# Five SBUF homes in place of three for the output tiles of a fused linear-attention and channel-mix kernel

## The chip, the core and the metric

The kernel runs on one NeuronCore of a Trainium2 chip. The metric is the device time of one launch in microseconds, the median of several runs. TensorE is called PE here (its weight loads PEld), VectorE DVE, ScalarE ACT, GpSimd POOL and SyncE SP. A trailing q (SPq, DVEq) marks work of an engine's sequencer: it waits or issues DMAs while the engine itself stays idle.

## The reference

Eight batches, eight heads, 576 positions, 64 numbers per head. An attention of linear kind feeds a channel mix:

```python
q_s = softmax(q, over the head's 64)
k_s = softmax(k, over the 576 positions)
x   = q_s @ (k_s^T @ v)                    # heads side by side: [8, 576, 512]
x_prev = x, one position later, 0 in front
xk = mu_k * x + (1 - mu_k) * x_prev
xr = mu_r * x + (1 - mu_r) * x_prev
k  = maximum(xk @ w_k, 0)                  # 512 -> 1024
v  = (k * k) @ w_v                         # 1024 -> 512
out = sigmoid(xr @ w_r) * v                # float32
```

## The kernel before

**Tiling.** `attention(b, g)` makes x for one batch and four heads. Exponentials (ACT, L454), sums and reciprocals (DVE, L467 and L470) and the scaling of q (DVE, L475) prepare its inputs. One block on PE, in tiles of 64x64, then transposes q (L507), forms the product of keys and values (L484, into a PSUM tile `att`) and multiplies q with the product of the block before it (L520). Between them DVE takes the reciprocal of the key sums (`rz`, L492), copies the transposed q out of PSUM (`qt`, L512) and scales the product into weights (`w`, L605); ACT copies x out in two pieces (`xb`, L614 and L617); DVE shifts, scales and mixes it (L622 to L636) into `xk` and `xr`, two bf16 rings of four batches.

The channel mix runs in units of 512 positions, the last of each half 256 (`unit`, L694). For each of eight slices of the 1024 hidden numbers, PE multiplies `xk` with `w_k` into one of four PSUM banks `mm_a` to `mm_d` (`k_part`, L722), ACT takes the RELU (`rel`, L706) and DVE squares it into `k2` (L710; the pages write k_a, k_b). Then, for each 128 positions, PE makes the gate's argument from `xr` and `w_r` (`r_part`, L756), ACT its tanh into a tile `th` (L761), and PE the value from `k2` and `w_v` in two halves of four matmuls (`v_part`, L766). DVE's `gated` (L772) adds 1 to the tanh and multiplies with the value in PSUM: it writes one output tile `ot` of 128 x 512 float32, 2 KB per partition, and by that sets the PSUM bank free. `store` (L783) sends the tile to HBM in two DMAs of 64 rows, 128 KB each, on SP's queue. There are 36 output tiles; the last is made and stored in two column halves, so 37 instructions are at L772.

**Order.** Nothing is ordered by a scheduler on the chip. `Plan` holds every operation with its engine, an estimated duration, what it depends on, and which buffers it takes and sets free. `Plan.order` books one operation at a time: for each engine, the one that can start first among those whose inputs are ready, and among those that can start within a look-ahead the one due first. Lead times such as `EARLY` are set by hand. The resulting order is emitted as it is, and each engine works through its queue in that order. Semaphore waits are put in for each dependence: on data, and on a buffer that an earlier reader still holds. An instruction with several things to wait for gets extra wait instructions ahead of it (EVENT_SEMAPHORE).

**Homes.** Each buffer family has a number of places, listed in `pools`. When an operation takes one, `slot_time` gives the place whose last user ends first:

```python
late = [o.end for o in user.last]
free = None if not late or None in late or free is None else max(
    [free] + late)
...
if free is not None and (best is None or free < best[0]):
    best = (free, i)
```

For `ot` the last users are the tile's stores. In the trace the homes `ot_a`, `ot_b` and `ot_c` are used in turn. So each `gated` waits on the chip until both DMAs of the tile three before it have landed, and DVE, which works in order, waits with it. The operations of SP in this phase are the stores alone; POOL issues the loads of q, k and v (`raw`, L310), the last of them at 98.95 us.

Of the kernel before, what the change touches and what calls it, by code (L numbers as in the profile page):

```python
# [208 lines left out]
def kernel(  # L209
# [25 lines left out]
    assert B % 4 == 0  # L235

    pools = {"raw": 12, "eq": 3, "ek": 2, "vv": 2, "stat": 4, "qs": 2, "qt": 3, "w": 3, "wp": 4,
             "rz": 3, "xb": 2, "xd": 2, "xm": 3, "k2": 2, "rel": 3, "th": 2, "ot": 3, "mm": 4,
             "att": 2, "early": 2}
    shared = {("early", i): [("mm", 2 * i), ("mm", 2 * i + 1)] for i in range(2)}  # L240
    plan = Plan(pools, shared)
# [620 lines left out]
```

## Time and profile before

Five runs: 201.1 to 202.66 us, median 202.21. The profiled execution took 201.58 us; its span, from the first instruction to the last, is 199.8 us. The granted PE clock was full (1.00) throughout.

| stretch, us | length | PE busy | DVE busy | ACT busy | POOL busy | DMA, GB/s |
|---|---|---|---|---|---|---|
| 0 to 20 | 20.0 | 9.88 | 12.84 | 12.00 | 10.44 | 261 |
| 20 to 95 | 75.0 | 73.91 | 67.34 | 65.08 | 29.04 | 358 |
| 95 to 112 | 17.0 | 16.26 | 15.03 | 12.31 | 1.44 | 195 |
| 112 to 187 | 75.0 | 74.21 | 61.04 | 43.78 | 0.00 | 57 |
| 187 to 199.8 | 12.8 | 8.72 | 4.56 | 3.96 | 0.00 | 83 |

A row gives the time in which each engine was busy within the stretch, and the mean rate of all DMAs. Up to about 105 us the loads of q, k, v and the weights share the DMA engines with the stores; after that only stores are left.

| stores (L783), each 128 KB | least | median | most |
|---|---|---|---|
| issue to landing, 30 to 110 us | 3.2 | 6.2 | 8.6 |
| issue to landing, 110 to 200 us | 2.2 | 2.4 | 3.7 |

A DMA's landing is the moment at which its semaphore has its full count. Times of matmuls overlap their neighbours' in the records, as they are pipelined and their ends are modelled; distances from start to start are the safer measure. In a timeline the bracket behind an instruction gives how long its engine sat idle before it, and the instruction that the profile names as having ended the wait.

### The profile page before, as it was taken

What the parts mean: (1) busy time and instruction counts of PE and PEld (TensorE: products, weight loads), DVE (VectorE), ACT (ScalarE), POOL (GpSimd) and SP (SyncE); (2) the same over time, 40 slices, a digit from 0 to 9 for tenths busy, and PEclk for the clock granted to TensorE, in tenths of its full rate; (3) what the DMA queues carried; (4) which work ended last, traced back from release to release, by engine and by line L of the source; (5) the groups of instructions that cost most, each with busy time, mean ns of one, the idle gap of its engine ahead of it and who ended that gap; (6) DMA issues with size and microseconds to landing.
All of it is one profiled execution on the core that took longest, in us unless ns stands there. A gap on an engine that the chain in (4) does not pass through costs nothing.

```text
span 199.8 us, 5314 instructions
## 1 busy us (share of the span) xinstructions
PE 183.0 (92%) x2147; PEld 96.4 (48%) x2171; DVE 160.8 (80%) x348; ACT 137.1 (69%) x212; POOL 40.9 (20%) x66
## 2 busy tenths in 40 slices
PE   2447999999999999999989999999999999999991
PEld 0234554545344555454466455455455544544761
DVE  2598668899999999999969999999998997432531
ACT  5493795998999699969559978846842652552440
POOL 1594365743345023312300000000000000000000
PEclk9999999999999999999999999999999999999999
DMA  6999999999999999992991220252042204402514
GB/s 213 360 248 223 298 266 359 390 402 410 391 402 411 404 401 382 400 386 66 267 362 37 54 56 0 53 113 50 3 106 56 53 3 105 105 0 58 118 37 105
DMA packets 15520, 40.72 MB, mean 204 GB/s; under 512 B 2300, under 2 KB 3592, under 8 KB 15496
## 3 DMA queue, kind: packets, MB, share of 16 engines
q0 software_dynamic: 7840, 27.40, 40.3%
q1 hardware_dynamic: 7208, 12.26, 21.3%
q10 hardware_dynamic: 448, 0.72, 1.2%
q8 instruction: 17, 0.28, 0.6%
q14 instruction: 7, 0.06, 0.1%
HBM read 33.56 MB, written 9.44 MB: 215 GB/s over the span
## 4 chain that ended last, share of the span: by engine, by line
PE 89%; DMA 4%; DVE 3%; issue 1%; ACT 1%
PE mm_c L766 10%; PE mm_a L722 10%; PE mm_d L722 9%; PE mm_d L766 8%; PE mm_a L766 7%; PE mm_c L722 7%; PE mm_b L766 6%; PE mm_b L722 6%; PE mm_b L756 6%; PE mm_d L756 4%; PE mm_c L756 3%; PE mm_a L756 3%; PE att_b L520 3%; DMA raw_d<-in_q_dram 3%; PE att_a L520 2%; PE att_b L507 2%
## 5 line engine op out<-in xcount | busy, mean ns | idle before, releaser
L722 PEld LDWEIGHTS <-wk 128*128 128x128 bf16 x320 | 35.4, 114 | 27.7 <-issue 1.9
L722 PE MATMUL mm_a<-xk,wk 128*128 128x512 bf16 (+1 forms) x96 | 23.9, 358 | 0.3 <-issue 0.2
L722 PE MATMUL mm_d<-xk,wk 128*128 128x512 bf16 (+1 forms) x87 | 22.4, 370 | 0.3 <-DVE ot_a L772 0.3
L766 PEld LDWEIGHTS <-k_b 128*128 128x128 bf16 x152 | 14.5, 98 | 15.7 <-issue 0.7
L756 PEld LDWEIGHTS <-xr 128*128 128x128 bf16 x144 | 13.9, 98 | 15.9
L766 PEld LDWEIGHTS <-k_a 128*128 128x128 bf16 x144 | 13.4, 98 | 15.5 <-issue 0.4
L722 PE MATMUL mm_c<-xk,wk 128*128 128x512 bf16 (+1 forms) x66 | 16.0, 358 | 0.4 <-issue 0.3
L722 PE MATMUL mm_b<-xk,wk 128*128 128x512 bf16 (+1 forms) x62 | 15.5, 352 | 0.2
L756 PE MATMUL mm_b<-wr_bf,xr 128*128 128x512 bf16 x50 | 13.2, 379 | 0.1
L766 PE MATMUL mm_c<-wv_bf,k_a 128*128 128x512 bf16 x46 | 12.1, 379 | 0.2 <-issue 0.2
L766 PE MATMUL mm_c<-wv_bf,k_b 128*128 128x512 bf16 x47 | 12.1, 379 | 0.2 <-issue 0.2
L761 ACT ACTIVATE th_a<-mm_b 128x512 f32<-128x512 f32 x12 | 7.1, 595 | 6.4 <-PE mm_b L756 4.9
L766 PE MATMUL mm_d<-wv_bf,k_b 128*128 128x512 bf16 x39 | 10.1, 379 | 0.2 <-issue 0.2
L766 PE MATMUL mm_b<-wv_bf,k_a 128*128 128x512 bf16 x38 | 10.0, 379 | 0.2 <-issue 0.2
L766 PE MATMUL mm_a<-wv_bf,k_b 128*128 128x512 bf16 (+1 forms) x39 | 9.2, 358 | 0.1
L756 PE MATMUL mm_d<-wr_bf,xr 128*128 128x512 bf16 x34 | 9.1, 379 | 0.1
L710 DVE TENSOR_TENSOR k_a<-rel_c 128x512 bf16<-128x512 bf16 (+1 forms) x13 | 5.1, 389 | 3.5 <-ACT rel_c L706 3.5
L766 PE MATMUL mm_d<-wv_bf,k_a 128*128 128x512 bf16 x28 | 7.5, 379 | 0.4 <-issue 0.3
L710 DVE TENSOR_TENSOR k_a<-rel_b 128x512 bf16<-128x512 bf16 (+1 forms) x14 | 5.6, 397 | 2.8 <-ACT rel_b L706 2.8
L761 ACT ACTIVATE th_b<-mm_c 128x512 f32<-128x512 f32 x6 | 3.7, 608 | 5.6 <-PE mm_c L756 4.7
L756 PE MATMUL mm_c<-wr_bf,xr 128*128 128x512 bf16 x28 | 7.2, 379 | 0.1
L756 PE MATMUL mm_a<-wr_bf,xr 128*128 128x512 bf16 x28 | 7.2, 379 | 0.0
(275 smaller groups left out, 416.3 us busy)
## 6 DMA issues: line engine op xcount, KB each, us to landing
out_dram<-ot_a SPq DMA_DIRECT2D x24, 128.0 KB, 3.5
out_dram<-ot_b SPq DMA_DIRECT2D x24, 128.0 KB, 3.0
out_dram<-ot_c SPq DMA_DIRECT2D x22, 128.0 KB, 2.9
raw_b<-in_k_dram POOLq DMA_DIRECT2D x3, 576.0 KB, 8.6
raw_c<-in_v_dram POOLq DMA_DIRECT2D x3, 576.0 KB, 8.1
raw_d<-in_q_dram POOLq DMA_DIRECT2D x3, 576.0 KB, 9.3
raw_a<-in_q_dram POOLq DMA_DIRECT2D x2, 576.0 KB, 10.1
raw_e<-in_k_dram POOLq DMA_DIRECT2D x2, 576.0 KB, 11.0
```

The costliest lines, as they stand in the source:

```text
L507: nc.tensor.transpose(out=transposed()[64 * u:64 * u + 64, hf, 64 * j:64 * j + 64], in_=qss[qs.index][r, j, 64 * u:64 * u + 64], identity= ...
L520: nc.tensor.matmul(bank(xp)[64 * hf:64 * hf + 64, u, at + c:at + e], lhsT=w[r, hf, :], rhs=qts[qt.index][r, hf, src:src + e - c], start=(n ...
L710: nc.vector.tensor_tensor(out=k2s[k2.index][:, fc, 0:n], in0=rels[rel.index][:, 0:n], in1=rels[rel.index][:, 0:n], op=ALU.mult)
L722: nc.tensor.matmul(bank(kf)[:, 0:n], lhsT=(w[:, h, u, fc % 4:F // 2:4] if split[ct // 2] else w[:, u, F // 2 * h + fc % 4:F // 2 * (h + 1) ...
L756: nc.tensor.matmul(bank(rps), lhsT=xs[1][:, ct, c:c + 128], rhs=wr_bf[:, ct // 2 + 2 * (ct % 2), :], start=(ct == 0), stop=(ct == CT - 1))
L761: nc.scalar.activation(out=ths[th.index][:], in_=bank(rps), func=ACT.Tanh, scale=0.5)
L766: nc.tensor.matmul(bank(vps)[:, 0:w], lhsT=k2s[k2.index][:, ft, 128 * m:128 * m + 128], rhs=wv_bf[:, ft, e:e + w], start=(ft == 0), stop=( ...
```

## The change

The output tiles get five homes, `ot_a` to `ot_e`, in place of three. `buffers("ot", ...)` makes as many tiles as `pools` says, and `slot_time` chooses among as many. No operation is added or taken away, and the order of the operations on every engine is the one of before. A `gated` then waits for the stores of the tile that had its home last; the homes are again taken in turn. The tiles take 10 KB per partition in place of 6 KB, and what is placed behind them in SBUF moves up by 4 KB per partition.

```diff
@@ -235,7 +235,7 @@
     pools = {"raw": 12, "eq": 3, "ek": 2, "vv": 2, "stat": 4, "qs": 2, "qt": 3, "w": 3, "wp": 4,
-             "rz": 3, "xb": 2, "xd": 2, "xm": 3, "k2": 2, "rel": 3, "th": 2, "ot": 3, "mm": 4,
+             "rz": 3, "xb": 2, "xd": 2, "xm": 3, "k2": 2, "rel": 3, "th": 2, "ot": 5, "mm": 4,
              "att": 2, "early": 2}
```

## The prediction

> **What bounds the kernel now.** I read the page first: engine shares, then the chain of work that ended last.
>
> ```profile
> PE 183.0 (92%) x2147; PEld 96.4 (48%) x2171; DVE 160.8 (80%) x348; ACT 137.1 (69%) x212; POOL 40.9 (20%) x66
> ...
> PE 89%; DMA 4%; DVE 3%; issue 1%; ACT 1%
> ```
>
> PE carries 89% of the chain, and the table by stages shows it busy 73.91 of 75 us (20 to 95 us) and 74.21 of 75 (112 to 187). An output home can only matter where the wait for it reaches PE. So I went to DVE, which writes the homes (L772), and asked for its waits between 100 and 107 us, where the chain leaves PE:
>
> ```profile
> DVE ot_a L772 <- ACT rel_a L706: 1.8, 1, 1.8
> ...
> PE att_a L520 <- ACT xb_a L617: 0.4, 1, 0.4
> ...
> PE mm_d L722 <- DVE ot_a L772: 0.3, 1, 0.3
> ```
>
> Columns: who waited, for whom, total us, times, longest. One gating instruction stood still for 1.8 us, and two PE waits follow from it. The named releaser can't be right by the code: L772 reads `th`, `mm` and writes `ot`; nothing of it depends on `rel`. So I looked at L772 between 98.7 and 103 us, and at the store (L783) that last read this home:
>
> ```profile
> L772 DVEq EVENT_SEMAPHORE  x2: 21/36/50, 99.7 to 102.4; - x2
> ```
>
> ```profile
> L783 SPq DMA_DIRECT2D out_dram<-ot_a x2: 467/532/596, 95.0 to 95.5; - x2
> ...
> DMA to landing us min/median/max: 4.6/5.7/6.8
> ```
>
> The two halves of the home's last store were issued at 95.04 and 95.55 us and took 4.6 and 6.8 us: they landed at 99.64 and 102.35. DVE's two wait instructions start at 99.7 and 102.4. Each is released where a half lands; the match at both ends is what I rest on.
>
> Here a rule decides between readings. By the releaser's name the wait is on ACT, the home is innocent, and the change is worth 0. Of the Trainium skill, "Perfetto Trace Analysis", section "Sequencer-only Instruction (DRAIN, etc)", says that the profiler's start of such an instruction is the moment at which its semaphores are satisfied. That is a statement on sequencer instructions in general, which I apply to these two; it makes the home the cause, worth the sum below. ACT's `rel_a` ends at 102.49 by coincidence.
>
> **The change, part by part.**
>
> *Two more homes.* No instruction is added; 2 x 512 x 4 = 4,096 bytes per partition are. All L772 and L783 stay, in their order. With homes in turn, the gate at 102.49 takes the home used five tiles before (gated at 81.24, its store's second half issued at 82.46 and 6.1 us in flight: landed 88.6). That lies 12 us ahead, so this wait goes.
>
> *The other 36 gates.* Before 110 us a half store takes 3.2 to 8.6 us to land, later 2.2 to 3.7 (median 2.4). The next tightest reuse before 110 us is the gate at 83.81: its home's last half was issued at 75.79 and took 6.3, landing at 82.1, 1.7 us early. After 110 us the tightest are 5.3 to 6.1 us from issue to gate, above 3.7. They give 0 here. The first five gates in place of three carry no store wait; two pairs of wait instructions of 21 to 50 ns, hidden in a DVE that is 90% busy there beside PE: 0.
>
> *What a rule says against it.* "DMA: Bandwidth & Descriptors", section "Anatomy of one DMA — SWDGE (gpsimd) path", fits a DMA on POOL's path at about 2.0 us + bytes / 436 GB/s; a half store, if SP's path is alike, of 131,072 bytes is then 2.3 us (an estimate from that page), landing at 97.9. By the rule three homes suffice and the sum is 0. The late rows agree (2.4 us); the rows at 95 us do not (4.6 and 6.8), as loads fill the DMA engines (413 GB/s between 100.7 and 102.5 us, share 1.06). I take the row.
>
> *What is late next on DVE.*
>
> ```profile
> 99.41 1.29 DVE L467 TENSOR_REDUCE rsum_a<-eq_a 128x18 f32<-128x1152 bf16 x1
> 102.49 0.69 DVE L772 SCALAR_TENSOR_TENSOR ot_a<-th_b,mm_d 128x512 f32<-128x512 f32 x1 [1.79 <-ACT rel_a L706]
> 103.10 0.28 DVE L710 TENSOR_TENSOR k_a<-rel_c 128x256 bf16<-128x256 bf16 x1
> 103.30 0.16 DVE L492 RECIPROCAL rz_a<-att_a 128x2 f32<-128x2 f32 x1
> 103.38 0.74 DVE L512 COPY qt_a<-att_a 128x1152 bf16<-128x1152 bf16 x1
> 104.03 0.28 DVE L605 TENSOR_TENSOR w_c<-att_a,rz_a 128x128 bf16<-128x128 f32 x1
> ```
>
> Columns: start, duration, instruction, idle time before. The other inputs are `mm_d` (its last matmul ends at 99.50 + 1.03 = 100.53) and `th_b` (ACT, done at 99.14). So the gate starts when DVE is free, at 99.41 + 1.29 = 100.70, 1.79 earlier. The square follows 0.61 later at 101.31. `rz_a` then needs the key-value product in `att_a` (PE, 101.02 + 0.49 = 101.51): 101.55. `qt_a` 101.63, `w_c` 102.28 to 102.56, and DVE stays 1.75 ahead.
>
> *What PE gets.*
>
> ```profile
> 99.50 1.03 PE L766 MATMUL mm_d<-wv_bf,k_b 128*128 128x512 bf16 x4
> 100.45 0.41 PE L520 MATMUL att_b<-qt_c,w_b 64*64 64x512 bf16 x4
> ...
> 101.91 0.60 PE L722 MATMUL mm_c<-xk,wk 128*128 128x256 bf16 x4
> 102.34 0.60 PE L722 MATMUL mm_b<-xk,wk 128*128 128x256 bf16 x4
> 103.23 0.60 PE L722 MATMUL mm_d<-xk,wk 128*128 128x256 bf16 x4 [0.29 <-DVE ot_a L772]
> 103.67 0.60 PE L722 MATMUL mm_a<-xk,wk 128*128 128x256 bf16 x4
> 104.66 0.41 PE L520 MATMUL att_a<-qt_a,w_c 64*64 64x512 bf16 x4 [0.40 <-ACT xb_a L617]
> ...
> 107.50 1.02 PE L766 MATMUL mm_a<-wv_bf,k_a 128*128 128x512 bf16 x4
> ...
> 110.95 1.19 PE L722 MATMUL mm_d<-xk,wk 128*128 128x512 bf16 x4
> 111.98 0.38 PE L766 MATMUL mm_b<-wv_bf,k_a 128*128 128x512 bf16 x1
> ```
>
> Ends are modelled, so I go from start to start. An undisturbed group of four 256-wide matmuls takes 102.34 - 101.91 = 0.43, of 512-wide 0.86; the change to 64x64 tiles adds 100.45 - 99.50 - 0.86 = 0.09.
> 1. To 103.23: 0.89 against 0.43. Bank `mm_d` was held by the gate. **0.46**.
> 2. To 104.66: 0.99 against 0.43 + 0.09. L520 waits for `w_c` and for ACT's L617. **0.47**. Next late: ACT's `rel_c`, which was queued behind the square, now waits for PE's `mm_b` (102.34 + 0.60 = 102.94) and starts at about 102.98; ACT's narrow RELUs start 0.27 apart, so L617 runs from 103.25 to 103.52. PE arrives at 102.77 + 0.86 + 0.09 = 103.72, with 0.16 to spare (0.20 less 0.04 of signalling): no new stall.
> 3. To 107.50: 0.95 from 106.55, where 0.86 is due. **0.09**. It waits for ACT's `rel_b` (107.05 + 0.40 = 107.45), late by the same queue; about 1.4 earlier after, where PE comes 1.0 earlier.
> 4. To 111.98: 1.03 against 0.86, for DVE's `xk` (110.73 + 0.76 = 111.49). **0.17**. `xk` comes 1.75 earlier, PE 1.02.
>
> Sum 0.46 + 0.47 + 0.09 + 0.17 = **1.19 us**. After 112 us I find no PE wait beyond tile changes of 0.09, so it is carried to the end.
>
> *What moves earlier with it.* The two store halves leave SP about 1.8 us sooner, 0.26 MB into a full DMA (0.26 / 0.413 = 0.63 us). The load they can delay, `raw_d` (issued 98.95, landed 105.3), is first read at 141.06: cover 35 us. SP holds only stores then, and POOL's last load is issued at 98.95, before the gate.
>
> The profiled execution took 201.58 (span 199.8, 1.8 around it), so 201.58 - 1.19 = 200.39. The runs' median is 202.21, 0.63 above it; the stall is no part of that difference that I can show, so I take 1.19 from the median: **201.0 us**.
>
> **Rivals.**
>
> *The stall is replaced in part.* Step 2 has only 0.16 us in hand on ACT. If L617 is late by what it lost before, step 1 alone remains with some of the rest: 0.2 to 0.7 us, 201.5 to 202.0. For it: ACT is in order and `ek_b` of 1.17 us follows. Against: that follows L617.
>
> *The home isn't the cause, or unprofiled runs land their stores in time.* The label says ACT; and 1.79 us of wait hang on one landing of 6.8 us, where 5.0 would have been in time. Then 202.2.
>
> *More than this.* If landings in other executions come as late as the slowest here, 8.6, the stall is 1.8 us longer, and the gate at 83.81 comes within 0.6 us of binding. PE would then gain up to 3.0: 199.2.
>
> *Slower: an order moves after all.* The plan ranks DVE's operations by when they can start, and a home's booked release is in that time, so with more homes a gate may rank earlier. Place: DVE between 100 and 106 us. If one 1.35 us `qs` or `rsum` operation lands ahead of `w_c`, L520 waits 1.35 less the 0.16 in hand, 1.2 us, and with the hand-set lead times off, elsewhere too: 203.4. It decides as soon as DVE's order before `w_c` grows by over 0.16 us. Against: the homes are never the last to come free except once, and the orders are said to stay.
>
> **How the numbers follow.** Under 0.5%, 1.01 us of 202.21, a measurement can't tell from no change. The forecast (gain 0.8 to 1.6) gets 0.58, of which 0.48 over the bound and 0.10 within; "more" 0.06, faster; "in part" 0.14 and "not the cause" 0.09, within; "slower" 0.13. Faster 0.54, same 0.33, slower 0.13. The range 200.2 to 202.3 reaches from a gain of 2.0 to no change; it leaves out the slower case and most of "more", under 0.2. The forecast's own range is 200.6 to 201.4.
>
> **What would show it.** In the profile after: the gate on `mm_d` near 100.7 us starts with no idle time, and the two wait instructions before it start together with it, not 2.7 us apart; PE's group on `mm_d` (L722) and L520 follow 0.43 and 0.52 after the one before; PE's later starts all stand about 1.2 us earlier. I am wrong if the gate still starts behind `rel_a`; if PE waits at L520 for L617 as long as before; if orders differ; or if the span shrinks by 1.2 but the runs' median doesn't.

## The result, and the profile after

| | runs | median | lowest to highest |
|---|---|---|---|
| before | 71 | 202.25 us | 200.63 to 203.94 |
| five homes | 36 | 201.14 us | 200.33 to 202.52 |

The ratio after to before is 0.9948, with a 95% interval of 0.9935 to 0.9960: 1.05 us less, between 0.8 and 1.3. The forecast was 201.0. Ratios here and below are of fast runs: a run more than 1.5% above the fastest of its kernel is left out of them.

The change did one thing more than the section on it says. The order of the operations was not the one of before. The plan books the homes too, and with five it moved operations. With the buffers' numbers left out, 12 of DVE's 348 instructions stand elsewhere in the order, 7 of ACT's 212 and 12 of PE's 2171 weight loads with their matmuls, all between about 42 and 77 us; from about 47 us on the PSUM banks are dealt out differently. What the moves are worth is one of the questions below.

The view that carried the prediction, the waits between 100 and 107 us, in the profile after:

```profile
POOL raw_d L310 <- ACT eq_b L454: 2.9, 1, 2.9
ACT xb_a L614 <- PE att_b L520: 0.8, 1, 0.8
PEld L520 <- issue: 0.6, 2, 0.4
ACT rel_c L706 <- PE mm_c L722: 0.6, 1, 0.6
ACT rel_a L706 <- PE mm_d L722: 0.2, 1, 0.2
```

That is the whole answer: no wait of DVE, none of PE. What is left belongs to engines with time to spare. DVE's timeline shows the gate itself:

```profile
100.03 1.29 DVE L467 TENSOR_REDUCE rsum_a<-eq_a 128x18 f32<-128x1152 bf16 x1
101.24 0.69 DVE L772 SCALAR_TENSOR_TENSOR ot_a<-th_b,mm_a 128x512 f32<-128x512 f32 x1
...
102.94 0.28 DVE L605 TENSOR_TENSOR w_c<-att_a,rz_a 128x128 bf16<-128x128 f32 x1
```

It follows the reduction with nothing between; before, 1.79 us lay there. Its wait instructions, from the view of L772 between 99.3 and 102 us:

```profile
L772 DVEq EVENT_SEMAPHORE  x2: 21/880/1739, 99.4 to 99.5; - x2
```

They now start 0.1 us apart. The prediction expected them to start together with the gate; they start 1.8 us ahead of it, and the second one lasts. Its 1,739 ns are spent on PE's value, 99.46 + 1.74 = 101.20, and covered by the reduction. PE over the same stretch:

```profile
102.97 0.60 PE L722 MATMUL mm_c<-xk,wk 128*128 128x256 bf16 x4
103.40 0.60 PE L722 MATMUL mm_a<-xk,wk 128*128 128x256 bf16 x4
103.84 0.60 PE L722 MATMUL mm_d<-xk,wk 128*128 128x256 bf16 x4
104.37 0.41 PE L520 MATMUL att_a<-qt_a,w_c 64*64 64x512 bf16 x4
...
106.26 1.03 PE L756 MATMUL mm_a<-wr_bf,xr 128*128 128x512 bf16 x3
107.12 1.03 PE L766 MATMUL mm_d<-wv_bf,k_a 128*128 128x512 bf16 x4
...
110.57 1.03 PE L722 MATMUL mm_a<-xk,wk 128*128 128x512 bf16 x4
111.44 0.81 PE L766 MATMUL mm_c<-wv_bf,k_a 128*128 128x512 bf16 x3
```

From start to start: 0.43, 0.44, 0.53, and further on 0.86 and 0.87. The four excesses of before (0.46, 0.47, 0.09, 0.17) are all gone.

**Why the two spans differ by half a microsecond only.** The profiled execution after took 201.25 us with a span of 199.3, 0.5 below the one before. As a landmark I take PE's first value matmul (L766), and as the end the last gate. From PE's and DVE's timelines of before:

```profile
30.67 1.03 PE L766 MATMUL mm_b<-wv_bf,k_a 128*128 128x512 bf16 x4
...
195.81 0.42 DVE L772 SCALAR_TENSOR_TENSOR ot_c<-th_b,mm_b 128x256 f32<-128x256 f32 x1 [0.40 <-PE mm_b L766]
```

And of after:

```profile
31.34 1.03 PE L766 MATMUL mm_b<-wv_bf,k_a 128*128 128x512 bf16 x4
...
195.28 0.42 DVE L772 SCALAR_TENSOR_TENSOR ot_a<-th_b,mm_c 128x256 f32<-128x256 f32 x1 [0.40 <-PE mm_c L766]
```

Before, 195.81 + 0.42 - 30.67 = 165.56 us lie between; after, 164.35. That is 1.21 less. The start of this execution was 0.67 us later, in a stretch in which no output tile exists yet. Below, profiles are compared from this landmark on.

### The profile page after: what moved, and what is told of

Read it like the earlier page. It is cut to its first block, busy times and chain, and to the rows that moved or that the text cites. A ratio compares the mean times of both kernels' runs of the same rounds, so it can differ in the third digit from the quotient of the medians.

```text
span 199.3 us, 5313 instructions
## 1 busy us (share of the span) xinstructions
PE 183.3 (92%) x2147; PEld 96.5 (48%) x2171; DVE 161.4 (81%) x348; ACT 136.8 (69%) x212; POOL 41.0 (21%) x66
## 4 chain that ended last, share of the span: by engine, by line
PE 90%; DMA 4%; DVE 2%; issue 1%; ACT 1%
PE mm_c L766 9%; PE mm_b L766 9%; PE mm_a L722 9%; PE mm_d L722 9%; PE mm_b L722 8%; PE mm_a L766 7%; PE mm_c L722 7%; PE mm_d L766 7%; PE mm_c L756 5%; PE mm_a L756 4%; PE mm_b L756 4%; PE mm_d L756 4%; PE att_b L520 3%; DMA raw_d<-in_q_dram 3%; PE att_a L520 3%; PE att_b L507 2%
## 5 line engine op out<-in xcount | busy, mean ns | idle before, releaser
L766 PEld LDWEIGHTS <-k_b 128*128 128x128 bf16 x152 | 14.4, 98 | 15.8 <-issue 0.7
L722 PE MATMUL mm_a<-xk,wk 128*128 128x512 bf16 (+1 forms) x83 | 21.2, 370 | 0.2 <-issue 0.2
L766 PEld LDWEIGHTS <-k_a 128*128 128x128 bf16 x144 | 13.4, 98 | 15.4 <-issue 0.2
L722 PE MATMUL mm_b<-xk,wk 128*128 128x512 bf16 (+1 forms) x79 | 19.8, 363 | 0.1
L766 PE MATMUL mm_c<-wv_bf,k_a 128*128 128x512 bf16 x52 | 13.9, 380 | 0.4 <-issue 0.3
L766 PE MATMUL mm_a<-wv_bf,k_b 128*128 128x512 bf16 x46 | 11.9, 379 | 0.3 <-issue 0.3
L756 PE MATMUL mm_c<-wr_bf,xr 128*128 128x512 bf16 x42 | 11.2, 380 | 0.1
L766 PE MATMUL mm_b<-wv_bf,k_b 128*128 128x512 bf16 x40 | 10.3, 379 | 0.0
L766 PE MATMUL mm_b<-wv_bf,k_a 128*128 128x512 bf16 x38 | 10.0, 379 | 0.2 <-issue 0.2
L761 ACT ACTIVATE th_a<-mm_c 128x512 f32<-128x512 f32 x10 | 6.0, 598 | 5.8 <-PE mm_c L756 4.6
L756 PE MATMUL mm_a<-wr_bf,xr 128*128 128x512 bf16 x35 | 9.2, 379 | 0.1
L761 ACT ACTIVATE th_b<-mm_b 128x512 f32<-128x512 f32 x8 | 4.8, 597 | 5.5 <-PE mm_b L756 4.8
L756 PE MATMUL mm_b<-wr_bf,xr 128*128 128x512 bf16 x32 | 8.2, 379 | 0.1
L766 PE MATMUL mm_d<-wv_bf,k_a 128*128 128x512 bf16 x32 | 8.2, 379 | 0.0
L706 ACT ACTIVATE rel_b<-mm_d 128x512 bf16<-128x512 f32 (+1 forms) x10 | 5.6, 560 | 3.1 <-PE mm_d L722 3.1
```

What stands on the lines that cost most here:

```text
L706: nc.scalar.activation(out=rels[rel.index][:, 0:n], in_=bank(kf)[:, 0:n], func=ACT.Relu, scale=HALF_ROOT)
L722: nc.tensor.matmul(bank(kf)[:, 0:n], lhsT=(w[:, h, u, fc % 4:F // 2:4] if split[ct // 2] else w[:, u, F // 2 * h + fc % 4:F // 2 * (h + 1) ...
L756: nc.tensor.matmul(bank(rps), lhsT=xs[1][:, ct, c:c + 128], rhs=wr_bf[:, ct // 2 + 2 * (ct % 2), :], start=(ct == 0), stop=(ct == CT - 1))
L761: nc.scalar.activation(out=ths[th.index][:], in_=bank(rps), func=ACT.Tanh, scale=0.5)
L766: nc.tensor.matmul(bank(vps)[:, 0:w], lhsT=k2s[k2.index][:, ft, 128 * m:128 * m + 128], rhs=wv_bf[:, ft, e:e + w], start=(ft == 0), stop=( ...
```

## Experiments

The theory: one gate, for the 16th tile, waits until its home's store has landed, and PE pays for this wait. The rivals: the moved order and banks carry the gain; the 4 KB shift of what lies behind the homes in SBUF carries it; several gates wait, each in some executions. All kernels keep the line numbers of before. Each was compared with runs of before on the same chip (medians 201.98 us for the first four, 201.73 for the others).

### The order of before, five homes

The plan still has `"ot": 3`; the homes are dealt out behind it.

```diff
-    plan = Plan(pools, shared)
+    plan = Plan(pools, shared); pools["ot"] = 5
...
-                             [ot] if e == 0 else [], [vps, th])
+                             [ot] if e == 0 else [], [vps, th]); e or tiles_out.append((o, ot))
...
-    for op in plan.order():
+    ops = plan.order()
+    tiles_out.sort(key=lambda t: t[0].start)
+    for n, (_, ot) in enumerate(tiles_out):
+        ot.index = n % 5
+    for op in ops:
```

> The plan is made with three homes, so every engine keeps the order and the PSUM banks of before; then the 36 output tiles are dealt to five homes in turn. The wait of one gate for its home carries the gain: the gate near 102.5 us starts about 1.8 us earlier, PE's L520 behind it 0.9 to 1.0 us earlier, ratio to before 0.994 to 0.995. The moved order of the changed kernel carries it: 0.999 to 1.001. The 4 KB shift in SBUF carries it: 0.994 to 0.995 too.

Median 201.12 us, ratio 0.9947 (0.9922 to 0.9972). Order and banks are those of before, and the gain is the same within the intervals. PE's timeline shows it behind the gate:

```profile
104.02 0.60 PE L722 MATMUL mm_d<-xk,wk 128*128 128x256 bf16 x4
104.45 0.60 PE L722 MATMUL mm_a<-xk,wk 128*128 128x256 bf16 x4
104.98 0.41 PE L520 MATMUL att_a<-qt_a,w_c 64*64 64x512 bf16 x4
```

Distances of 0.43 and 0.53 again, now with `mm_d` and `mm_a` in the roles of before. The moved order is not needed for the gain. The shift in SBUF is in this kernel too; the next one has the shift without the gain.

### The new order, three homes

The same edit with 5 in the plan, five homes placed and `ot.index = n % 3`.

> The plan is made with five homes (order and banks of the changed kernel), five are placed in SBUF, but the tiles are dealt to three of them in turn. The wait carries the gain: the gate near 102 us waits again for 1.5 to 2 us until its home's store lands, ratio 0.999 to 1.001. The moved order or the shift in SBUF carries it: 0.994 to 0.995, although the gate waits.

Median 204.29 us (202.18 to 207.99), ratio 1.0105 (1.0077 to 1.0133). Neither expectation names that: the gain is lost, so neither order nor shift carries it, and 2 us more are lost. The profile is of the fastest of the 14 runs; the median lies 2.1 us above it, and what the longer runs lose beyond the waits below is not shown. From its list of waits:

```profile
DVE ot_a L772 <- DMA out_dram<-ot_a: 2.2, 1, 2.2
...
DVE ot_a L772 <- ACT xb_a L614: 1.2, 1, 1.2
```

The second is the 16th gate, as expected. The first is the fourth gate, and DVE's and PE's timelines show its price:

```profile
42.53 0.69 DVE L772 SCALAR_TENSOR_TENSOR ot_a<-th_b,mm_c 128x512 f32<-128x512 f32 x1 [2.20 <-DMA out_dram<-ot_a]
43.14 0.75 DVE L577 CAST xk<-att_a 128x576 bf16<-128x576 f32 x1
```

```profile
43.94 0.44 PE L520 MATMUL att_a<-qt_a,wp_d 64*64 64x288 bf16 x8 [1.36 <-DVE xk L577]
```

Before, this gate ran at 51.85; the new order has it at 42.1, ahead of a copy for which PE waits. With five homes that is free. With three, it waits for a store issued at 36.1 that lands at 42.4, and PE waits 1.36 us. The eighth gate waits 0.52 us in the same way. So the order of before had three homes built into it: the plan books the homes, and it had put these gates later.

### One tile spared

The order of before, four homes placed, `ot.index = 3 if n == 15 else n % 3`: only the 16th tile has a home of its own.

> Order and banks of before, three homes in turn, but the one tile whose gate waited (the 16th) goes to a fourth home. One gate is the whole cause: ratio 0.994 to 0.995, as with five homes for all. Several gates wait in runs that no profile showed: a smaller gain, 0.996 to 0.999. The order is the cause: 1.000.

Median 201.40 us, ratio 0.9962 (0.9941 to 0.9984). By the runs alone that is undecided: the interval holds the full gain and a smaller one. In the profile the gate follows the reduction without idle time. From DVE's timeline:

```profile
100.70 1.30 DVE L467 TENSOR_REDUCE rsum_a<-eq_a 128x18 f32<-128x1152 bf16 x1
101.93 0.69 DVE L772 SCALAR_TENSOR_TENSOR ot_d<-th_b,mm_d 128x512 f32<-128x512 f32 x1
```

No other gate waits for a store in this profile, and from the landmark to the end it takes 164.42 us, as with five homes (164.41 in the same order). So this one gate accounts for the whole difference between the profiles. That another gate waits in some of the unprofiled runs is not excluded: the 12th is the next, and its home's store landed 0.67 us ahead of it here, 1.7 us in the profile before, 0.36 us in the kernel of "A longer wait".

### Four homes

The order of before, `ot.index = n % 4`.

> Order and banks of before, tiles dealt to four homes in turn. The 16th gate then waits for a store that landed near 92 us, 8 us before it: one more home is enough, ratio 0.994 to 0.995. If the fifth home matters too: 0.996 to 1.000.

Median 200.97 us, ratio 0.9964 (0.9948 to 0.9980), 164.43 us from the landmark. The ratio lies above the 0.994 to 0.995 expected if one more home is enough, in the range named for a fifth home that matters (0.996 to 1.000); its interval includes 0.995, so the runs don't decide. In the profile no gate waits for a store, and nothing is left for a fifth home to give.

### The loads held back

Three homes and the order of every engine as before, but the last three loads wait for the 15th gate. On top of the edit above, with 3 in place of 5 and L772 returning its instruction:

```diff
-    for op in ops:
+    held = loaded[7, 1, 0][0] + loaded[7, 1, 1][0] + loaded[7, 1, 2][0]
+    after = tiles_out[14][0]
+    ops = [o for o in ops if o not in held]
+    at = ops.index(after) + 1
+    for op in ops[:at] + held + ops[at:]:
         op.made = op.emit()
+        if op in held:
+            tc.add_manual_dep(op.made.ins, after.made.ins.name, sync)
```

> Three homes as before, order of every engine as before, but the last three loads (raw of the last four heads, issued at 94.3, 95.4 and 98.9 us before) wait on POOL for the gate of the tile before (near 99.3 us). The loads make the store late: the 16th tile's home lands 2.5 to 4 us after issue in place of 6.8, its gate starts near 100.7 with no wait, ratio 0.994 to 0.996. The store is slow of itself: it still takes 6 us or more, ratio 1.000.

Median 201.17 us, ratio 0.9960 (0.9942 to 0.9977): most or all of the gain, with three homes. The view of L783 between 95.2 and 96.2 us has the store that the 16th gate waits for, the one between 101.5 and 102.5 us a later store:

```profile
L783 SPq DMA_DIRECT2D out_dram<-ot_a x2: 466/531/596, 95.4 to 95.9; - x2
...
DMA to landing us min/median/max: 2.2/2.3/2.4
```

```profile
L783 SPq DMA_DIRECT2D out_dram<-ot_a x2: 467/634/802, 101.6 to 102.2; - x2
...
DMA to landing us min/median/max: 7.3/7.4/7.5
```

The same kind of store takes 2.2 to 2.4 us with these three loads out of its way, and 7.3 to 7.5 where they now run, issued at 99.92 to 101.33. The loads make the landing late. The busy share of the DMA engines does not tell the two cases apart: between 95 and 99 us it is 0.90 here and 0.98 before, as the stores and the end of one earlier load (`raw_i`, issued at 92.88, 4.1 us in flight) keep them busy too. In DVE's timeline the gate has no idle time left:

```profile
99.72 1.29 DVE L467 TENSOR_REDUCE rsum_a<-eq_a 128x18 f32<-128x1152 bf16 x1
100.93 0.69 DVE L772 SCALAR_TENSOR_TENSOR ot_a<-th_b,mm_d 128x512 f32<-128x512 f32 x1
```

### A longer wait

The order of before, three homes, `ot.index = 1 if n == 15 else n % 3`: the 16th tile takes the home of the 14th.

> Order and banks of before, three homes, but the 16th tile takes the home of the tile two before it, whose store lands about 1.6 us later (103.1 to 104.2 us). PE has no slack left behind this gate, so a longer wait costs PE its full length: ratio 1.006 to 1.009 (1.2 to 1.8 us). If PE has other work to pull forward or the wait is hidden in part: 1.000 to 1.004.

Median 202.65 us, ratio 1.0051 (1.0033 to 1.0069). The wait grew by less than expected. From DVE's timeline:

```profile
103.06 0.69 DVE L772 SCALAR_TENSOR_TENSOR ot_b<-th_b,mm_d 128x512 f32<-128x512 f32 x1 [2.47 <-DMA out_dram<-ot_b]
```

It is 2.47 us, not 3.4, as the later store landed only about 0.7 us behind the earlier one; so the ratio lies between the two expectations. What the longer wait adds, PE pays, as the table below shows.

### Both kernels profiled again

No edit.

> The kernel of before, profiled a second time. The landing that the gate waits for is set by the traffic of the loads, so it is late again: a wait of 1.3 to 2.3 us at the gate near 102 us. If the first profile caught a chance: under 0.5 us.

> The changed kernel, profiled a second time. No wait at the gate near 101 us again, PE's starts behind it apart by 0.43 and 0.53 us. Its first 20 us tell how far the start alone moves between executions: if PE's first matmul with the weights of the channel mix and its start of the second unit differ from the first profile's by 0.3 us or more, the start and not the change made up the other half microsecond between the two spans.

In the second profile of before, DVE's timeline has the wait again:

```profile
102.47 0.69 DVE L772 SCALAR_TENSOR_TENSOR ot_a<-th_b,mm_d 128x512 f32<-128x512 f32 x1 [1.27 <-ACT xb_a L614]
```

It is 1.27 us in this execution, as the second half of its store took 6.3 us in place of 6.8. That lies just under the expected 1.3 to 2.3 and far above the 0.5 named for a chance: the wait is there again, and its length varies with the landing. Of the four PE delays, the first was gone and the others had 0.41, 0.09 and 0.17 us. After had no wait again, and 164.35 us from the landmark to the end as in its first profile, but a span of 200.2 us: its matmuls with `wk` near 18 us came 0.65 us later than in the first profile, its landmark 0.94. By the sign named in the expectation, the start and not the change made the other half microsecond.

### All profiles together

| kernel | wait of the 16th gate | landmark | landmark to end | above 164.40 |
|---|---|---|---|---|
| after | none | 31.34 | 164.35 | |
| after, again | none | 32.28 | 164.35 | |
| old order, five homes | none | 31.90 | 164.41 | |
| one tile spared | none | 31.95 | 164.42 | |
| four homes | none | 31.76 | 164.43 | |
| loads held | none | 30.98 | 164.41 | |
| before, again | 1.27 | 31.17 | 165.05 | 0.65 |
| before | 1.79 | 30.67 | 165.56 | 1.16 |
| a longer wait | 2.47 | 30.54 | 166.26 | 1.86 |
| new order, three homes | 1.23, and 2.20 and 0.52 at others | 29.94 | 166.65 | 2.25 |

The six profiles without the wait, of five kernels, agree within 0.08 us, with three, four or five homes placed, two orders, two sets of banks: neither order nor placement is worth more than that once no gate waits. In the three with the order of before that wait, the wait less what PE lost is 0.62, 0.63 and 0.61 us. So about 0.62 us of the wait are covered, and between 1.27 and 2.47 us everything beyond is paid in full; no run has a shorter wait. The prediction's sum says the same: 1.79 - 1.19 = 0.60.

## Why the prediction was right

**The cause** was read rightly. The profile named ACT's `rel_a` as the releaser (ACT's `xb_a` in the second profile of before); the starts of the two wait instructions named the store. Sparing the one tile, or hastening the one store, took the wait away, and `rel_a` was left as it was. What the prediction took from a page on these starts, that all semaphores are satisfied then, holds only in part: with two semaphores the instruction started at the first that it names, as the 1,739 ns above show. Here the store's is named first, so the reading came out right.

**The sum.** 1.19 us was forecast against the profiled execution; from the landmark on it is 1.21. Each of the four terms went, and none came back elsewhere. The runs gained 1.05 us (0.8 to 1.3, which includes 1.19), and in the experiments that take the wait away 0.58 to 0.86 us between medians. The term that varies is the wait's length: 1.79 us in one execution, 1.27 in another. I took the one profiled wait for the usual one; from the second profile of before the same comparison gives 0.70 us (165.05 to 164.35). That the number for the runs came so close is therefore in part luck: the mechanism is shown, the usual length of the wait is not.

**What is late next** was the closest call, 0.16 us in hand at L617. ACT's timeline after has it:

```profile
103.88 0.26 ACT L617 CAST xb_a<-att_a 128x128 bf16<-128x128 f32 x1
```

It ends at 104.14, and PE starts L520 at 104.37, on time. The rival of a stall replaced in part did not come.

**The rule on DMAs** (about 2.3 us for a half store, an estimate from the page "DMA: Bandwidth & Descriptors", section "Anatomy of one DMA — SWDGE (gpsimd) path", of the Trainium skill) was rightly put behind the row. With the three loads held back the store took 2.2 to 2.4 us, just that; among the loads its second half took 6.3 to 6.8. Here the rule gives the price without these loads, and the loads decided.

**The slower rival** came half true, and not where I put it. An order did move, though I had counted on the description that it doesn't, and had named differing orders as a sign of being wrong. It moved before 77 us, not between 100 and 106, and cost nothing: the ratio with the new order is 0.9948, with the old one 0.9947. It becomes dear only where the new order meets the old number of homes.

**One reading was wrong** in the rival of a larger gain: a landing after 8.6 us would come at 75.79 + 8.6 = 84.39, so the gate at 83.81 would not come within 0.6 us of waiting, it would wait for 0.6. The latest landing seen there took 7.67 us ("A longer wait") and left 0.36.

**Still open**: why the start differs. The landmark lies between 29.94 and 32.28 us in ten profiles, a spread of 2.3 us, twice the gain. PE's timelines show where most of it arises: early in the launch the same matmuls take longer, and the end of that stretch moves. Between 18 and 23.4 us, before:

```profile
18.58 1.06 PE L722 MATMUL mm_d<-xk,wk 128*128 128x512 bf16 x2
...
20.70 0.59 PE L722 MATMUL mm_b<-xk,wk 128*128 128x512 bf16 x2
```

And after:

```profile
20.41 1.04 PE L722 MATMUL mm_a<-xk,wk 128*128 128x512 bf16 x2
...
22.68 0.62 PE L722 MATMUL mm_c<-xk,wk 128*128 128x512 bf16 x2
```

The traces' records of the granted clock begin only at 19.73 us before and at 21.81 after, so the full clock "throughout" in the section on the time before is shown from there on alone. In the ten profiles they begin at 18.92 to 20.59 us in the five whose tiles use three homes, at 21.81 to 23.15 in the five that use more, and the landmarks are sorted in the same way (29.94 to 31.17, and 31.34 to 32.28). No output tile exists at that time, and why it sorts so, if it isn't chance, is not shown. In the profiles the start works against the gain, so it didn't carry it there; in the other runs the start can't be seen.

## What to carry to other kernels

An output home is needed for as long as its store takes to land under the traffic of that moment, not on an idle queue: where loads and stores share the DMA engines, compare the slowest landing of that stretch with the time in which the homes come round, in a burst of tiles above all. At the one place that these runs show, three tiles came round in 6.4 us (gates at 94.33 and 100.70, where DVE was free), while the home was taken for 8.0 us (from 94.33 to the landing at 102.35). That this holds elsewhere was not tested. A wait that the profile puts down to an engine which the instruction doesn't read is settled by laying the start of its wait instructions beside the landings of the DMAs that hold its output. And an order made with a number of buffers belongs to that number: change both together, as the new order on three homes lost what the extra homes had gained and 2 us more.

## What I had not expected of the hardware

In one kernel ("The loads held back") a 128 KB store took 2.2 us without three 576 KB loads beside it and 7.5 us with them, while the busy share of the DMA engines was 0.90 even in the first case. The landing that the 16th gate waits for took 6.8 us in one execution of before and 6.3 in the next; a wait that hangs on it has no fixed length. A wait instruction with two semaphores started when the first that it names was satisfied, and spent its duration on the second: the one ahead of the 16th gate, which names the store's before PE's, lasted 50 ns before, where the store came last, and 1,739 ns after, where PE did.
